# Attention and two gated layers on one core: weights rounded from 8 bytes with fewer VectorE and more ScalarE operations, and a written issue order for the whole program

## The chip, the cores and the metric

The kernel runs on one core of one Trainium2 chip. The metric is the device time of one execution in microseconds, from runs of the whole program. The engines are TensorE (matrix products, PE in the profile), VectorE (DVE), ScalarE (ACT), GpSimd (POOL) and SyncE (SP, which issues most transfers). Each engine executes its own instructions in the order in which they were issued, and engines wait for each other by semaphores.

## The reference

Three stages follow each other. The first is attention with a window of 128 positions and a linear distance bias, for 4 sequences of 576 positions and 8 heads of 64; its result is read as 2304 tokens of width 512. The second is a gated layer of inner width 1536, the third a product of two projections of inner width 1024, a square matrix and an output matrix.

```python
x = attention(q, k, v)                        # 2304 x 512
gate = 1.0 / (1.0 + np.exp(-(x @ w_gate)))
x = gate * (x @ w_val) @ w_out                # inner width 1536
a = x @ w1
b = x @ w2
h = a * b @ w3                                # inner width 1024
return (h @ w_out2).astype(np.float32)
```

The weights arrive as 8-byte floating-point numbers; the kernel takes each apart as two 4-byte words, `low` and `high`, and makes a 4-byte number of them. That is called a rounding below. Every operand of a large product is then split in a high part and a remainder, and each product is three matmuls (high x high, high x remainder, remainder x high).

## The kernel before, in words

The 2304 tokens are five blocks of 2, 4, 4, 4 and 4 tiles of 128. The attention phase runs over 20 steps (5 blocks x 4 pairs of heads) as a pipeline written for TensorE: scores (`stage_s`, L817), then on the other engines mask (L826), bias (L830), maximum (L838, L842), exponentials on ScalarE (L846), sums and reciprocals (L850, L851), normalizing (L856 on GpSimd, L858 on ScalarE); then transposes (`stage_p`, L867) with a copy to SBUF on ScalarE (L106, tile `cp`) and masks on GpSimd (L873, L877); then the product with the values (`stage_pv`, L892). Steps 2 and 3 take their keys and queries from one tile, `boot`, which three transfers fill (L787 to L789). Between the steps TensorE gets pieces of the second stage (`fill`).

The second stage runs over 12 slices of the inner width in groups of two, and for each group over the blocks: the products gate and value (`gv`, L422), a tanh (L437), the gated product on VectorE (L444), its split on ScalarE and GpSimd (L106, L112), then the output product (`dn`, L462) with its addition on VectorE (L470, L472). The third stage first folds `w3` and `w_out2` into one matrix (L383), keeps it in DRAM, and then forms the products by a scheme with seven block products in place of eight (`products`, L533), with operands made by `form_part` and `x_forms`, and the output (`down2`, L663).

Weights are fetched by SyncE (L172, L175) into a ring, rounded by `rounded` (L197 on ScalarE, L199 to L204 on VectorE) and either split into a weight tile (`c`), kept as a form, or stored to DRAM as 4 bytes for later (L217). 76 pieces of 128 x 512 weights are rounded.

Three things set the order. TensorE's order in the attention phase is the program's. The order of the other four engines in the attention phase and shortly after it is written out in the strings of `TURNS`: one letter per instruction, and `line_up` ties each instruction to the one before it in the string. Letters are e for an exponential, n for normalizing, p for the copy of transposes, o for the split of a value product, m, t, x, s for mask, bias, maximum and sum, a and r for the rounding's ScalarE and VectorE instructions, c for the weight's split, g, y and d for tanh and gated product, its split, and the addition; on SyncE k, b, v, w and u for the transfers of keys and queries, `boot`, values, weights, and stores. After the attention phase a scheduler orders every engine by priorities (`high_priority`, `issue_after`).

Of the kernel before, what the change touches and what calls it, by code (L numbers as in the profile page):

```python
# [27 lines left out]
F64_LEAST = 0x38000000  # L28
F64_MOST = 0x47EFFE00
# [9 lines left out]
        "hhmtxmtxsxsrmrtrxsxsrmtrxsxsrmmtsosrxtrxrmsosrtmsxsxtrxrsxrsomrtosxsxmtrxrsxsrrmsstoxmxtgxxrssrm"  # L39
        "sstmxtxorssrmsstmxoxtrxrsmsxotmxsrsxrtrxrxsrsrromstmxrsgddxdtrxrsxrdsrmrtsmsxortrxrgsrsrsmsodddt"  # L40
        "mxtxrdrxrsxrsmotsmsxtxrxrrxsrsrmormgsdddstdrxrxtrxrmrxrsrsrtosxgsmddtsxdssmstoxmxtxxsmsdtomxsxst"
        "ssxxmotxgsdxmdtsdsdsxxsosgdddoorrdrdddgrdrrrrgdrdrrrddgdddd"
    ),
    mybir.EngineType.Activation: (
        "khThhThhaeeeeennepepeaeneehnpepeeeeocnnnnppoeeeepeeeeapnnonneeeepeopeeenngnneepeeceeeneopnnancpe"
        "eeeeeeeopnnnnpeeeeepeeennnnyopaeeeepoceeenneagneeneeepeoeepcnnannyepeeeeneeoenpgnnecepeepeeeenon"
        "nnapeoeeepyeeeenannngpeeeeeoeeenpnnanyeeeppeeoeegneneeenneppeeeeonnnnpeeeeoeepnneegnenepeeypneen"
        "oeeeyeeenngenpeoeepnnnppyooagcaccycgccygy"
    ),
    mybir.EngineType.Pool: (  # L50
        "hhhihhhhhhhhhhhhhThiTnnzzzznnzzhTnzznTnnTzzzczznzznznnTTnzznzTnnzzncnnznzzczzTnnnnzzTzznznnnTzyz"
        "zznncznnnzTzncnnzzznzynnnzzzznnzncnzTzzznzynnnznzTTzTnznnznynznnzzzzznnnnznznzzznnznnyzznznnznzy"
        "znznzzzzycccyccycy"
    ),
    mybir.EngineType.SP: (
        "kkkkkbwbbkvwkvvvkkkwkkvkvkwkkvkwkvvkkkwwvkvkkwkkvkkvuwvkkkuwkkkvuukvkvvvkvwwwwww"
# [26 lines left out]
def attn_moe_kernel(  # L83
# [106 lines left out]
    def rounded(t, key):  # L190
# [89 lines left out]
    def form_part(i, c, x):  # L280
# [3 lines left out]
        def split(at, src):  # L284
            hi, lo = w[:, at : at + 2, 0], w[:, at : at + 2, 1]
            act_copy(hi, src)
            pool_lo(lo, src, hi)
# [845 lines left out]
```

## Time and profile before

| | before |
|---|---|
| median of 3 runs | 879.13 us (879.13 to 880.4) |
| span of the profiled execution | 878.4 us |
| TensorE busy | 863.3 us, 4448 matmuls |
| VectorE busy | 654.0 us, 1161 instructions |
| ScalarE busy | 349.1 us, 853 instructions |
| GpSimd busy | 300.1 us, 357 instructions |
| TensorE idle in the first 88 us | 10.5 us |

The span runs from the first to the last instruction of one profiled execution; the runs' time is taken around the whole execution, and their median stands 0.7 us above it. A line of an engine's busy time tells how much of the span it worked; which engine set the end is read from what TensorE waited for and from the windows.

### The profile page before, as it was taken

What the parts mean: (1) busy time and instruction counts of PE and PEld (TensorE: products, weight loads), DVE (VectorE), ACT (ScalarE), POOL (GpSimd) and SP (SyncE); (2) the same over time, 40 slices, a digit from 0 to 9 for tenths busy, and PEclk for the clock granted to TensorE, in tenths of its full rate; (3) what the DMA queues carried; (4) which work ended last, traced back from release to release, by engine and by line L of the source; (5) the groups of instructions that cost most, each with busy time, mean ns of one, the idle gap of its engine ahead of it and who ended that gap; (6) DMA issues with size and microseconds to landing.
All of it is one profiled execution on the core that took longest, in us unless ns stands there. A gap on an engine that the chain in (4) does not pass through costs nothing.

```text
span 878.4 us, 12512 instructions
## 1 busy us (share of the span) xinstructions
PE 863.3 (98%) x4448; PEld 713.4 (81%) x4448; DVE 654.0 (74%) x1161; ACT 349.1 (40%) x853; POOL 300.1 (34%) x357
## 2 busy tenths in 40 slices
PE   6999999999999999999999999999999999999998
PEld 4677777788888888888888788888888888888887
DVE  6999996699988986993999955873558877643445
ACT  6998776433223223322322333432433334222110
POOL 4877555544135123313311211122555431111120
PEclk8999999999999999999999999999999999999999
DMA  5545540423722430530355421158325355654322
GB/s 186 174 160 179 179 154 16 144 95 115 244 74 83 151 127 24 170 132 1 105 191 168 159 85 54 67 180 318 137 84 180 109 216 216 217 179 155 134 82 97
DMA packets 40767, 121.67 MB, mean 139 GB/s; under 512 B 4480, under 2 KB 6784, under 8 KB 38656
## 3 DMA queue, kind: packets, MB, share of 16 engines
q1 hardware_dynamic: 39264, 105.92, 35.7%
q10 hardware_dynamic: 1440, 14.94, 4.0%
q8 instruction: 35, 0.57, 0.3%
q14 instruction: 28, 0.23, 0.1%
HBM read 88.34 MB, written 32.51 MB: 138 GB/s over the span
## 4 chain that ended last, share of the span: by engine, by line
PE 86%; DVE 6%; DMA 3%; issue 1%; ACT 1%; POOL 1%; SPq 0%; ACTq 0%; DVEq 0%
PE gv L422 28%; PE dn L462 15%; PE o L663 11%; PE pb L533 10%; PE pd L533 5%; PE w3o L383 5%; PE pv L892 3%; PE s L817 3%; PE lone L632 3%; PE pc L533 2%; PE pt L867 2%; DMA boot<-in_q_dram 1%; DVE acc L472 1%; DMA aw_('ahead', 15, 0)_4822<-in_w_dram 1%; DMA _('ahead', 'w3', 4)_5168<-in_w_dram 1%
## 5 line engine op out<-in xcount | busy, mean ns | idle before, releaser
L422 PE MATMUL gv<-xth,wsl 128*128 128x512 f32 (+1 forms) x960 | 279.6, 370 | 1.5 <-DVE g L444 1.5
L422 PEld LDWEIGHTS gv<-xth,wsl 128*128 128x128 f32 x960 | 174.6, 188 | 35.6 <-DVE g L444 2.1
L422 PE MATMUL gv<-xtl,wsl 128*128 128x512 f32 (+1 forms) x480 | 176.8, 368 | 0.0
L112 POOL TENSOR_TENSOR gt<-g,gt 128x512 fp32r<-128x512 f32 (+1 forms) x60 | 74.6, 1246 | 246.1 <-ACT gt L106 241.2
L462 PE MATMUL dn<-gt,wsl 128*128 128x512 f32 (+1 forms) x720 | 155.1, 369 | 0.4 <-DVE g L444 0.4
L462 PEld LDWEIGHTS dn<-gt,wsl 128*128 128x128 f32 x720 | 125.8, 189 | 24.3 <-ACT sm L858 0.7
L422 PEld LDWEIGHTS gv<-xtl,wsl 128*128 128x128 f32 x480 | 90.5, 189 | 14.6
L533 PE MATMUL pb<-xf,forms 128*128 128x512 f32 x384 | 97.7, 391 | 0.0
L472 DVE TENSOR_TENSOR acc<-acc,dn 128x512 f32<-128x512 f32 (+1 forms) x120 | 73.5, 625 | 16.7 <-PE dn L462 16.6
L533 PEld LDWEIGHTS pb<-xf,forms 128*128 128x128 f32 x384 | 70.8, 188 | 14.8 <-ACT xa L106 0.5
L106 ACT ACTIVATE gt<-g 128x512 fp32r<-128x512 f32 (+1 forms) x60 | 35.1, 586 | 78.7 <-DVE g L444 78.7
L846 ACT ACTIVATE sm<-sm,mn 128x128 f32<-128x128 f32 x144 | 56.0, 392 | 10.1 <-DVE mn L842 8.5
L673 DVE TENSOR_TENSOR acc<-acc,o 128x512 f32<-128x512 f32 (+1 forms) x54 | 36.5, 678 | 31.3 <-PE o L663 31.2
L444 DVE SCALAR_TENSOR_TENSOR g<-g,gv 128x512 f32<-128x512 f32 (+1 forms) x60 | 37.4, 627 | 29.3 <-PE gv L422 29.0
L533 PE MATMUL pd<-xf,forms 128*128 128x512 f32 x192 | 48.8, 389 | 0.0
L663 PE MATMUL o<-outw,tp 128*128 128x512 f32 x192 | 48.0, 390 | 0.0
L663 PE MATMUL o<-outw,tq 128*128 128x512 f32 (+1 forms) x192 | 47.6, 386 | 0.0
L112 POOL TENSOR_TENSOR tp<-x,tp 128x512 fp32r<-128x512 f32 x15 | 20.5, 1367 | 78.9 <-ACT tp L106 78.8
L437 ACT ACTIVATE g<-gv 128x512 f32<-128x512 f32 (+1 forms) x60 | 32.0, 547 | 32.3 <-PE gv L422 25.6
L383 PE MATMUL w3o<-wo,w3s 128*128 128x512 f32 x192 | 44.0, 389 | 0.0
L663 PEld LDWEIGHTS o<-outw,tp 128*128 128x128 f32 x192 | 36.0, 188 | 8.0 <-DVE tp L109 0.3
L533 PEld LDWEIGHTS pd<-xf,forms 128*128 128x128 f32 x192 | 36.0, 188 | 7.5
(808 smaller groups left out, 1445.7 us busy)
## 6 DMA issues: line engine op xcount, KB each, us to landing
formd<-forms ACTq DMA_DIRECT2D x8, 1792.0 KB, 6.0
outw<-outd SPq DMA_DIRECT2D x16, 512.0 KB, 5.0
forms<-formd SPq DMA_DIRECT2D x8, 1024.0 KB, 5.1
ldk<-in_k_dram SPq DMA_DIRECT2D x16, 320.0 KB, 2.9
ldv<-in_v_dram SPq DMA_DIRECT2D x16, 320.0 KB, 3.7
out_dram<-acc SPq DMA_DIRECT2D x17, 256.0 KB, 2.0
ldq<-in_q_dram SPq DMA_DIRECT2D x16, 256.0 KB, 3.9
outd<-w3o SPq DMA_DIRECT2D x8, 512.0 KB, 2.9
```

The costliest lines, as they stand in the source:

```text
L106: return nc.scalar.activation(dst, src, AF.Copy)
L112: nc.gpsimd.tensor_tensor(dst, src, hi.bitcast(F32), ALU.subtract)
L383: nc.tensor.matmul(acc2, w3s[u][:, wp, i * P : (i + 1) * P], wo2[kk][:, xp], start=(kk == 0 and wp == 0 and xp == 0), stop=(kk == NC2 - 1 ...
L422: nc.tensor.matmul(ps, wsl[i][:, s, wp, kk * P : (kk + 1) * P], xs[blk][xp][:, kk], start=(kk == 0 and wp == 0 and xp == 0), stop=(kk == N ...
L437: nc.scalar.activation(g[i], pss[i, 0], AF.Tanh, scale=0.5)
L444: nc.vector.scalar_tensor_tensor(pr, pr, 1.0, pss[i, 1], ALU.add, ALU.mult)
L462: nc.tensor.matmul(ps, wsl[i][:, 2, wp, m * P : (m + 1) * P], t[:, xp], start=n == 0, stop=n == 3 * len(grp) - 1,)
L472: nc.vector.tensor_tensor(a, a, ps, ALU.add)
L533: nc.tensor.matmul(ps, forms[i][:, a, wp, kk * P : (kk + 1) * P], xf[n, j][:, xp, kk], start=first and kk == 0 and (wp, xp) == PASSES[0], ...
L663: nc.tensor.matmul(ps[:, c], ts2[n, i][blk][:, xp, tt * P : (tt + 1) * P], outw[i][:, wp, c], start=k == 0, stop=k == 3 * len(grp) - 1,)
L673: nc.vector.tensor_tensor(a, a, ps[:, c], ALU.add)
L846: nc.scalar.activation(y, y, AF.Exp, bias=mn[:, j : j + 1], scale=1.0 / up, accum_out=sums[:, j, 0:1])
```

## The change

The rounding is rewritten: the scaling of the high word and the scaling of the low word are each one ScalarE operation, and VectorE clamps, joins the sign and joins the two words. The second temporary gets two buffers (`bufs=2`), the ring of 4-byte weights three instead of four. All instructions after the attention phase get letters too (F, X, P, L, D, f, K, O, A, Z, l and more of the old ones; q, r, R and j belong to the rounding), the strings run to the end of the program, and `line_up` is called there. TensorE's order is the program's all the way. The scheduler's priorities and `issue_after` give way to the letters.

```diff
-F64_LEAST = 0x38000000
-F64_MOST = 0x47EFFE00
+MOST = 0x0FEFFE00
+LOW_SCALE = 7.49 * 2.0**-32
...
     mybir.EngineType.Activation: (
-        "khThhThhaeeeeennepepeaeneehnpepeeeeocnnnnppoeeeepeeeeapnnonneeeepeopeeenngnneepeeceeeneopnnancpe"
+        "kThhhhTeeheeheenneejpapncnapoeeepejeeeennonnppppeeeeeeeneonnoneeeeppeeeennnceneeepegeeeponnjjnnppaee"
+        "eeeeneenconnppeeeeeeeennoynnaeepeeeopeeeanjnngeeneppeeoeneejcnncnjyppaeeeeeeeenonganneepepeoeceeejnn"
...
     mybir.EngineType.SP: (
-        "kkkkkbwbbkvwkvvvkkkwkkvkvkwkkvkwkvvkkkwwvkvkkwkkvkkvuwvkkkuwkkkvuukvkvvvkvwwwwww"
+        "kkbkkkbbwvvkwkkvvwkkkwvkkvkkvkkvwkkvvwkkvwkvkkwkkwukvkwkkkvukvukkuvkvkkvvvwwwwwwwwwwwwwwwuwuwwuuwwuu"
...
         a = (capool or spool).tile([P, DM], U32, name=f"a_{key}", tag="ca", bufs=rings["ca"])
-        s = spool.tile([P, DM], U32, name=f"s_{key}", tag="cs", bufs=1)
-        x, y = a.bitcast(F32), s.bitcast(F32)
+        s = spool.tile([P, DM], U32, name=f"s_{key}", tag="cs", bufs=2)
+        x = a.bitcast(F32)
         with turn("a"):
-            nc.scalar.activation(x, high.bitcast(F32), AF.Abs)
+            nc.scalar.activation(x, high.bitcast(F32), AF.Copy, scale=2.0**-112)
+        with turn("j"):
+            nc.scalar.activation(s, low, AF.Copy, scale=LOW_SCALE)
+        with turn("q"):
+            nc.vector.tensor_scalar(x, x, -bits(MOST), bits(MOST), ALU.max, ALU.min)
         with turn("r"):
-            nc.vector.tensor_scalar(x, x, bits(F64_LEAST), bits(F64_MOST), ALU.max, ALU.min)
-            nc.vector.tensor_scalar(a, a, 0x07FFFFFF, 3, ALU.bitwise_and, ALU.logical_shift_left)
-            nc.vector.scalar_tensor_tensor(a, high, 0xC0000000, a, ALU.bitwise_and, ALU.bitwise_or)
-            nc.vector.tensor_scalar(s, a, 0xFF800000, None, ALU.bitwise_and)
-            nc.vector.scalar_tensor_tensor(y, low, 2.0**-52, y, ALU.mult, ALU.mult)
-            nc.vector.tensor_tensor(x, x, y, ALU.add)
+            nc.vector.scalar_tensor_tensor(s, high, 0x80000000, s, ALU.bitwise_and, ALU.bitwise_or)
+        with turn("R"):
+            nc.vector.scalar_tensor_tensor(a, a, 3, s, ALU.logical_shift_left, ALU.bitwise_or)
...
-    rings.update({"raw": 3, "raw32": 4, "ca": 4})
+    rings.update({"raw": 3, "raw32": 3, "ca": 4})
...
+    ctx.enter_context(tc.manual_schedule(engines={mybir.EngineType.PE}))
     fillers += [layer(groups[0], 4), layer(groups[1], 3), layer(groups[1], 4)]
...
     while queue:
         convert_next()
-    line_up()
...
     for _ in downs:
         pass
+    line_up()
```

## Rows read from the trace of the kernel before

**Rows 1.** The page: busy us (share) and instructions; speed of transfers in 40 slices.
```profile
PE 863.3 (98%) x4448; PEld 713.4 (81%) x4448; DVE 654.0 (74%) x1161; ACT 349.1 (40%) x853; POOL 300.1 (34%) x357
...
GB/s 186 174 160 179 179 154 16 144 95 115 244 74 83 151 127 24 170 132 1 105 191 168 159 85 54 67 180 318 137 84 180 109 216 216 217 179 155 134 82 97
```
**Rows 2.** Windows of 22 us: each engine's busy us (instructions), granted clock, DMA share, GB/s.
```profile
0.00:22.00 22.00, 13.95 (x70) 9.29 (x71) 13.78 (x32) 13.78 (x53) 10.68 (x41) 0.84 0.56 186
22.00:44.00 22.00, 20.53 (x153) 15.02 (x153) 21.27 (x55) 21.39 (x83) 19.43 (x38) 1.00 0.51 175
44.00:66.00 22.00, 21.36 (x155) 15.52 (x155) 21.28 (x52) 21.17 (x81) 17.41 (x31) 1.00 0.45 159
66.00:88.00 22.00, 21.65 (x174) 17.53 (x175) 21.61 (x54) 19.18 (x69) 16.49 (x26) 1.00 0.54 180
```
**Rows 3.** Windows of TensorE alone, in two long stretches.
```profile
150.00:480.00 330.00, 330.00 (x1616) 1.00 0.35 119
506.00:862.00 356.00, 356.00 (x1670) 1.00 0.41 148
```
**Rows 4.** TensorE's waits: total us, times, longest.
```profile
PE s L817 <- DMA boot<-in_q_dram: 3.8, 1, 3.8
...
PE gv L422 <- DVE g L444: 1.5, 1, 1.5
```
**Rows 5.** The chain that ended last: start us, us, what.
```profile
216.15 5.44 PE dn L462 x24
221.59 10.88 PE gv L422 x48
```
**Rows 6.** TensorE's timeline in the attention phase: start us, us, line, tiles, count, idle before.
```profile
11.23 2.08 PE L817 MATMUL s<-boot 64*128 64x256 f32 x8 [3.76 <-DMA boot<-in_q_dram]
...
43.15 1.03 PE L867 MATMUL pt<-ident,sm 128*128 128x128 f32 x8
...
48.26 0.66 PE L867 MATMUL pt<-ident,sm 128*128 128x128 f32 x2
49.17 1.51 PE L867 MATMUL pt<-ident,sm 128*128 128x128 f32 x6 [0.24 <-POOL sm L856]
...
72.81 0.62 PE L462 MATMUL dn<-gt,wsl 128*128 128x256 f32 x3 [0.35 <-DVE g L444]
```
**Rows 7.** VectorE's timeline near 480 us.
```profile
477.74 0.42 DVE L199 TENSOR_SCALAR _('ahead', 'w3', 9)_5234<-_('ahead', 'w3', 9)_5234 128x512 f32<-128x512 f32 x1
...
479.35 0.69 DVE L201 SCALAR_TENSOR_TENSOR _('ahead', 'w3', 9)_5234<-_('ahead', 'w3', 9)_5204,_('ahead', 'w3', 9)_5234 128x512 uint32<-128x512 uint32 x1
...
483.11 1.52 DVE L200 TENSOR_SCALAR a_('w3', 6)_5562<-a_('w3', 6)_5562 128x512 uint32<-128x512 uint32 x1
484.55 0.68 DVE L204 TENSOR_TENSOR _('ahead', 'w3', 9)_5234<-_('ahead', 'w3', 9)_5234,_('ahead', 'w3', 9)_5235 128x512 f32<-128x512 f32 x1
485.15 0.67 DVE L444 SCALAR_TENSOR_TENSOR g<-g,gv 128x512 f32<-128x512 f32 x1
```
**Rows 8.** GpSimd's timeline at the same place.
```profile
482.73 1.61 POOL L112 TENSOR_TENSOR gt<-g,gt 128x512 fp32r<-128x512 f32 x1 [14.78 <-ACT gt L106]
```
**Rows 9.** ScalarE's first weight instruction, and VectorE's first maximum.
```profile
7.56 0.69 DVE L838 TENSOR_REDUCE mn<-sm 128x4 f32<-128x512 f32 x1
...
9.57 0.66 ACT L197 ACTIVATE a_(0, 0)_208<-raw_(0, 0)_129 128x512 f32<-128x512 f32 x1 [4.67 <-DMA raw_(0, 0)_129<-in_w_gate_dram]
10.14 0.39 ACT L846 ACTIVATE sm<-sm,mn 128x128 f32<-128x128 f32 x1
```
**Rows 10.** ScalarE's busy time from its first exponential to 22 us.
```profile
10.14:22.00 11.86, 10.22 (x45) 0.71 0.43 144
```
**Rows 11.** SyncE's timeline: start us, us of the issue, line, tile.
```profile
3.60 0.47 SPq L175 DMA_DIRECT2D raw_(0, 0)_129<-in_w_gate_dram  x1
```
**Rows 12.** The chain that ended last: the last boot transfer.
```profile
4.59 6.40 DMA boot<-in_q_dram
```
**Rows 13.** ScalarE's waits for transfers: total us, times, longest.
```profile
ACT _('ahead', 'w3', 2)_5170 L197 <- DMA _('ahead', 'w3', 2)_5144<-in_w_dram: 7.8, 1, 7.8
```

More of the change, by code (lines that the diff above doesn't have):

```diff
@@ L285, in split @@
             hi, lo = w[:, at : at + 2, 0], w[:, at : at + 2, 1]
-            act_copy(hi, src)
-            pool_lo(lo, src, hi)
+            with turn("F"):
+                act_copy(hi, src)
+                pool_lo(lo, src, hi)
         split(A11 if c == 0 else A21, x)
@@ L308, in keep @@
         r = (i - NF) * P
-        nc.scalar.dma_start(formd[r : r + P, :], forms[i][:, 1:].rearrange("p b h c -> p (b h c)").bitcast(F32))
+        with turn("K"):
+            nc.scalar.dma_start(formd[r : r + P, :], forms[i][:, 1:].rearrange("p b h c -> p (b h c)").bitcast(F32))
     def out_tile(i):
@@ L473, in down1 @@
             if last:
-                act_copy(x2[blk][0][:, m], a)
-                dve_lo(x2[blk][1][:, m], a, x2[blk][0][:, m])
+                with turn("X"):
+                    act_copy(x2[blk][0][:, m], a)
+                    dve_lo(x2[blk][1][:, m], a, x2[blk][0][:, m])
             yield 3 * len(grp) * (cols(blk) / 2.4 + 13.3)
@@ L558, in products @@
         with now():
-            copied = act_copy(x1, b)
+            act_copy(x1, b)
         if n == 0 and i == NF + 1:
-            make_forms(i + 1, copied)
+            make_forms(i + 1)
         while late:
-            with now(), tc.issue_after(copied.ins):
+            with turn("L"):
                 late.pop(0)()
@@ L569, in products @@
         with now():
-            copied = act_copy(x2a, b)
+            act_copy(x2a, b)
         if n == 0:
-            with tc.issue_after((copied if i > NF + 1 else folded[NM - 1]).ins):
-                keep(i)
+            keep(i)
         yield 2
@@ L576, in products @@
         with now():
-            copied = act_copy(x2b, b)
-            added = nc.vector.tensor_tensor(x2b, x2b, d, ALU.add)
+            act_copy(x2b, b)
+            nc.vector.tensor_tensor(x2b, x2b, d, ALU.add)
         while rests:
-            with tc.issue_after(added.ins):
-                rests.pop()()
+            rests.pop()()
         if n == 0 and NF + 1 < i < NF + NM - 1:
-            make_forms(i + 1, copied)
+            make_forms(i + 1)
         yield 0
@@ L592, in products @@
             nc.vector.tensor_tensor(x1, x1, b, ALU.mult)
-            ts[PAIRED[n][0]] = turn(x1, "tp", dve_lo if n and final else pool_lo)
+            ts[PAIRED[n][0]] = turned(x1, "tp", dve_lo if n and final else pool_lo)
         yield 1
@@ L611, in products, with make_forms @@
         yield 1
-    def make_forms(i, after):
-        with tc.issue_after(after.ins):
-            waiting.pop(i)()
+    def make_forms(i):
+        waiting.pop(i)()
         for c in range(2):
@@ L635, in lone @@
                     )
-            with tc.high_priority(offset=SOONER):
+            with turn("l"):
                 if s == 0:
@@ L668, in down2 @@
                     a = acc[blk][:, tt, c]
-                    with tc.high_priority(offset=SOONER):
+                    with turn("D"):
                         if grp[0] == NF:
@@ L675, in down2 @@
                         r0 = (STARTS[blk] + tt) * P
-                        (nc.scalar if c.start else nc.sync).dma_start(out[r0 : r0 + P, c], a)
+                        with turn("Z"):
+                            (nc.scalar if c.start else nc.sync).dma_start(out[r0 : r0 + P, c], a)
                 yield
```

73 lines of the change are left out of this document (47 added, 26 removed).

## Prediction

> **What bounds the kernel now.** I read the busy shares first, then the windows, then what TensorE waited for, then the places themselves. TensorE is busy 863.3 us of a span of 878.4, VectorE 654.0 [rows 1]: 15.1 us of TensorE's span are idle, so nothing that only relieves VectorE can bring more than about that. The windows say where the 15.1 us lie. From 150 to 480 us and from 506 to 862 us TensorE has no idle time [rows 3]. In the first 88 us the four windows leave it 8.05, 1.47, 0.64 and 0.35 us [rows 2], 10.5 in sum; one wait of 1.5 us lies near 485 us [rows 4]; the last 3 us are the tail (the last matmul, its addition, the last store), which the change leaves alone.
>
> A busy TensorE is not always at its pace, since the ends of matmuls are modelled; the pace is seen where a block repeats: 48 matmuls of 512 columns in 10.88 us [rows 5], 226.7 ns each. All the later blocks keep it. In the attention phase they do not: a block of eight transposes takes 1.03 us at 43.15, and from 48.26 to the end of its second row at 50.68 us where two of the eight ran ahead [rows 6], 1.3 us more. There are six such places between 20 us and the last of them at 72.81 us [rows 6]. Counted from start to start against an undisturbed block of the same kind they cost 0.9, 1.5, 1.0, 1.3, 0.8 and 0.6 us, 6.1 us in sum, of which only a part shows as idle.
>
> So what can be won lies in three places: the boot transfer at the start (3.8 us of waiting [rows 4]), these six stalls, and the one wait at 485 us. In the stretch of the stalls VectorE is busy 21.27, 21.28 and 21.61 us of 22 and ScalarE 21.39, 21.17 and 19.18 [rows 2]: both are nearly full, and the change moves work from one to the other.
>
> **The change, part by part.**
>
> *The rounding.* An undisturbed VectorE instruction of the forms at L199, L200 and L202 takes 0.42 us, one of L201, L203 and L204 0.69 us [rows 7]: six of them 3.33 us. The new three are one of the first kind (the clamp, same form as L199) and two with two inputs (same form as L201): 0.42 + 0.69 + 0.69 = 1.80 us. Each rounding gives VectorE back 1.53 us. Seven of the 76 roundings lie in the first 88 us: 7 x 1.53 = 10.7 us there. The other 69 give back 106 us, in stretches where TensorE is not idle at all [rows 3]: that is worth nothing unless it removes the wait at 485 us.
>
> *The added ScalarE instruction.* The conversion of the low word has no row of its own (whole-number input and output). The nearest row is the one beside it, which reads every second word of the same source: 0.66 us [rows 9]; queued behind another, an instruction starts some 0.1 us before the end of the one before, 0.57 us net. I take 0.57 to 0.68 us. Whether converting the type costs more no row shows; that it costs less is excluded by the same 512 elements per partition. Off the start it is hidden: 69 x 0.66 = 46 us, of ScalarE's time after 88 us that is mostly idle. At the start it is not. By the order strings the changed kernel has, when the 88th of the 144 exponentials has been issued, 9 first instructions (a), 9 of the new ones (j) and 6 copies of rounded weights (c) behind it, 24 in all, where the kernel before has 8 and 6. Ten more are 5.7 to 6.8 us on an engine that has 0.61 + 0.83 + 2.82 = 4.3 us free from 22 to 88 us [rows 2].
>
> *ScalarE's head start.* Before, the first thing behind the set-up on ScalarE is the rounding's first instruction; it waits 4.67 us for its weights and the exponentials stand behind it until 10.14 us, though the maximum that the first of them needs is ready at 8.25 us [rows 9]. In the new string four exponentials stand ahead of any weight: 1.9 us gained. Between 10.14 and 22 us ScalarE is busy 10.22 of 11.86 us [rows 10], 1.6 us free. Free in all: 4.3 + 1.9 + 1.6 = 7.8 us; taken: 5.7 to 6.8 us. The attention chain can come forward by 1.0 to 2.1 us where ScalarE is the limit, by more where VectorE was.
>
> *SyncE's order.* The first weight slice (512 KB) was issued at 3.60 us [rows 11], ahead of the last two boot transfers, the last at 4.59 us and landing 6.40 us later [rows 12]. Now all three boot transfers stand ahead of it, one of them between the loads of the first two steps. The last one is issued one slot (0.5 us) earlier with 512 KB less ahead of it. If transfers land in order, that is worth up to 1.6 us more at 318 GB/s, the fastest of the page's slices [rows 1]; if they share the engines, nothing. I take 1.2 us for both (bounds 0 and 2.1). The loads of the second step come one slot (0.5 us) later; VectorE is still at the first step then, which hides it. The weights land no earlier than before, and VectorE needs them later.
>
> *The stalls.* VectorE has 10.7 us more, SyncE brings the boot step 1.2 us sooner, ScalarE allows 1.0 to 2.1 us. Ends: nothing (ScalarE eats it) and 6.1 + 2.1 = 8.2 us (all six stalls and the boot). I take 2.5 us, near ScalarE's end, as it is the engine whose load grows.
>
> *The wait at 485 us.* TensorE waits 1.54 us for the gated product (L444) at 485.15 us. It stands in VectorE's queue behind L200, 1.52 us long where others take 0.42, and L204, 0.68 us [rows 7]. Both instructions are gone in the changed kernel. 2.2 us ahead of it against a wait of 1.5: I take the whole 1.5 us. Ends: 0 and 1.54.
>
> The long L200 started at 483.11 us, while a GpSimd subtraction ran from 482.73 for 1.61 us [rows 8]; it ended 0.3 us after that one, as if it had stood still. The Trainium skill (SBUF — State Buffer, section "Who interferes with whom") says that VectorE's two-port forms, and its instructions with two SBUF inputs, share a port pair with GpSimd, and that the loser blocks for the whole of the other's instruction; the row agrees (1.10 us lost). By that rule the three new instructions can all still be blocked, and the wait at 485 us would keep up to 1.1 us.
>
> *The order of everything else.* TensorE's own order is the program's in both: before, 24 dn and 48 gv follow each other as the loops are written [rows 5]. For the other engines the order after the attention phase was the scheduler's and is now a string. The buffers for 4-byte weights go from four to three, so the second load of a pair waits one form longer; the second temporary of the rounding lets two roundings overlap. With no idle time on TensorE from 506 to 862 us there is nothing to win there, only to lose: bounds 0 and the loss of the third rival. I take 0.
>
> *Sum.* 878.4 - 2.5 - 1.5 = 874.4 us of span. The median of the runs, 879.13, stands 0.7 us above the profiled span; with it 875.1 us.
>
> **The rivals.**
>
> *VectorE was the limit alone* (0.13). All six stalls and the boot's 2.1 us go, with the wait at 485: 6.1 + 2.1 + 1.5 = 9.7 us, 869.4 us. For it: VectorE's 21.3 to 21.6 of 22 us. Against it: ScalarE is as full.
>
> *Half the wait at 485 stays* (0.09). One of the new instructions is blocked beside GpSimd ahead of L444 as L200 was: 1.1 us come back, 876.2 us.
>
> *ScalarE takes VectorE's place* (0.18). Its ten more instructions use all that is free up to the 88th exponential; stalls move from 20 to 73 us to 65 to 95 us and nothing is won there. Only the wait at 485 goes: 877.6 us. The point from which it decides: an added instruction of over 0.75 us, or exponentials that don't start before 10 us.
>
> *A weight instruction at the head of ScalarE's queue* (0.16, slower). After the attention phase ScalarE's order is now fixed, with two instructions per load (a and j) instead of one that must wait for a transfer. Before, such waits reached 7.8 us [rows 13] and cost nothing, because the tanh that empties a bank had 10.88 us of matmuls ahead of it [rows 5] and the scheduler could place around them. Where the string puts tanh (g) or the gated copies (y) behind a load that lands later than that, TensorE stands still. It decides when wait and queue together pass some 10 us. Four such places at the price of the one in the trace, 1.54 us, are 6.2 us: 878.4 - 2.5 + 6.2 - 1.5 + 0.7 = 881.3 us. For it: the one wait of before is of this kind, at the end of the densest run of weights. Against it: VectorE's queue, which caused that one, gets shorter.
>
> **How the numbers follow.** The forecast 875.1 us gets 0.44 (its own range 872 to 877.3), the rivals 0.13, 0.09, 0.18 and 0.16. About 0.2% (1.8 us) is what a measurement here can tell from no change: faster is below 877.4 us. Faster: 0.44 + 0.13 + 0.09 = 0.66; same: 0.18; slower: 0.16. The range reaches from the large gain to the slower case, 869.5 to 881.0 us; outside are about half of each, 0.07 and 0.09.
>
> **What would show it.** Right: VectorE's busy time near 654 - 76 x 1.53 = 538 us or a little below, ScalarE's near 349 + 76 x 0.66 = 399; the boot step's matmuls near 10.0 us (11.23 before [rows 6]); the first exponential near 8.3 us; the transposes' blocks of 48 us at 1.0 us each; no wait for L444 near 480 us; TensorE still without idle time from 150 to 860 us. Wrong: an added ScalarE instruction above 0.75 us; ScalarE at 22 of 22 us from 44 to 88 us with TensorE waiting for it; any new wait of TensorE after 150 us; a boot step that starts at 11 us again.

## The result, and the profile after

The change made the kernel slower: 886.31 us (885.88 to 888.29, 4 runs) against 879.76 us (879.13 to 880.44), a ratio of 1.0076 with a 95% interval of 1.0062 to 1.0091. Forecast were 875.1 us and a range up to 881.0 us.

The page of the changed kernel, busy time and instructions of each engine, to be read beside [rows 1]:

```profile
span 886.6 us, 12284 instructions
...
PE 869.8 (98%) x4448; PEld 715.4 (81%) x4448; DVE 538.4 (61%) x933; ACT 387.5 (44%) x929; POOL 299.1 (34%) x357
```

VectorE lost 115.6 us of work, as forecast (538 us busy), and the span grew by 8.2 us. The profiled execution is the slowest of the four of the changed kernel; between the medians the loss is 6.6 us. Less work and more time can both be true only if VectorE's work was not what TensorE waited for. What TensorE did wait for (total, times, longest), to be read beside [rows 4]:

```profile
PE pt L891 <- POOL sm L880: 6.7, 8, 1.3
PE s L841 <- DMA ldk<-in_k_dram: 3.8, 1, 3.8
PE pb L559 <- ACT xa L119: 1.0, 2, 0.7
```

The wait for the boot transfer (3.8 us) and the one for the gated product near 485 us (1.5 us) are both gone. In their place stand eight waits of TensorE's transposes for the normalized exponentials (`sm`, L880), 6.7 us, all in the attention phase. The windows, to be read beside [rows 2] and [rows 3] (columns as there):

```profile
0.00:22.00 22.00, 15.95 (x60) 9.67 (x62) 12.03 (x25) 13.56 (x48) 11.62 (x42) 1.00 0.64 206
22.00:44.00 22.00, 19.83 (x146) 13.48 (x142) 17.45 (x45) 20.02 (x83) 15.62 (x35) 1.00 0.47 153
44.00:66.00 22.00, 18.98 (x148) 13.62 (x147) 19.00 (x43) 20.11 (x72) 14.36 (x28) 0.92 0.51 172
66.00:88.00 22.00, 22.00 (x170) 18.04 (x172) 20.21 (x48) 21.10 (x73) 17.25 (x30) 1.00 0.44 149
480.00:506.00 26.00, 26.00 (x139) 22.55 (x138) 10.12 (x16) 6.60 (x12) 5.15 (x4) 1.00 0.00 1
506.00:862.00 356.00, 354.81 (x1662) 296.81 (x1661) 205.63 (x316) 120.23 (x219) 98.00 (x76) 1.00 0.46 164
```

From 22 to 66 us VectorE is idle for 4.6 and 3.0 us of each window where it was idle for 0.7 before, ScalarE for 2.0 and 1.9 where it was idle for 0.6 and 0.8: no engine is full, and TensorE still idles more. From 480 to 506 us it is never idle. From 506 to 862 us, where it had no idle time, 1.2 us appear.

One landmark serves for all kernels below: a block of 16 score matmuls near the end of the attention phase. It starts at 121.02 us in the kernel before and at 128.35 us in the changed one:

```profile
121.02 2.00 PE L817 MATMUL s<-ldk,ldq 64*128 64x256 f32 x16
```
```profile
128.35 2.00 PE L841 MATMUL s<-ldk,ldq 64*128 64x256 f32 x16
```

So 7.3 us are lost by then. The wait near 485 us gives back 1.9 us (measured below). The last matmuls stand 7.7 us later than before (882.17 against 874.48 us), so 2.3 us are lost again in between. The rest of the 8.2 us, 0.5 us, lies behind the last matmul.

**Where the first loss begins.** VectorE's timeline of the changed kernel (start, us, line, tiles, and the idle time before with what ended it):

```profile
13.14 0.16 DVE L874 TENSOR_REDUCE su<-summed 128x4 f32<-128x8 f32 x1 [2.22 <-ACT sm L870]
13.22 0.69 DVE L850 COPY_PREDICATED s<-mask,s 128x512 f32<-128x512 int32 x1
...
22.10 0.70 DVE L850 COPY_PREDICATED s<-mask,s 128x512 f32<-128x512 int32 x1 [1.17 <-PE s L841]
...
23.32 0.68 DVE L850 COPY_PREDICATED s<-mask,s 128x512 f32<-128x512 int32 x1
23.91 0.15 DVE L874 TENSOR_REDUCE su<-summed 128x4 f32<-128x8 f32 x1
```

The boot step's scores begin at 8.29 us, but their mask stands behind the sum of step 1, which waits 2.22 us for ScalarE; the mask runs at 13.22 us, where it ran before (13.35). Later the sum of step 2 stands behind the masks of step 4, and these wait for TensorE's scores. ScalarE at the same time:

```profile
16.34 0.63 ACT L119 ACTIVATE wsl<-a_(0, 0)_208 128x512 fp32r<-128x512 f32 x1 [1.29 <-DVE a_(0, 0)_208 L218]
...
17.17 0.65 ACT L210 ACTIVATE a_(0, 1)_316<-raw_(0, 1)_131 128x512 f32<-128x512 f32 x1
18.82 0.38 ACT L119 ACTIVATE cp<-pt 128x256 f32<-128x256 f32 x1 [1.00 <-PE pt L891]
...
19.36 0.40 ACT L870 ACTIVATE sm<-sm,mn 128x128 f32<-128x128 f32 x1
```

The split of the rounded weight waits 1.29 us for VectorE, a copy waits 1.00 us for TensorE, and the exponentials of step 2 behind both start at 19.36 us (16.41 before). TensorE's transposes of that step start at 25.27 us (22.73 before):

```profile
19.99 2.93 PE L841 MATMUL s<-ldk,ldq 64*128 64x256 f32 x16
...
25.27 0.90 PE L891 MATMUL pt<-ident,sm 128*128 128x128 f32 x4 [1.24 <-POOL sm L880]
...
51.07 0.33 PE L891 MATMUL pt<-ident,sm 128*128 128x128 f32 x1 [0.70 <-POOL sm L880]
52.72 2.02 PE L891 MATMUL pt<-ident,sm 128*128 128x128 f32 x7 [1.32 <-POOL sm L880]
```

The last two rows are step 7's. An engine that executes its queue in order stands still for an instruction that nobody needs yet, while one that TensorE needs is ready behind it. That is the theory. The Trainium skill (PSUM — Partial Sum Buffer, section "Engine vs sequencer instructions") says that the queues of ScalarE, VectorE and GpSimd are strictly first in, first out; the 2.22 us agree with it.

The first row shows a rival for a part of this first loss, TensorE's own pace: step 4's sixteen score matmuls take 2.93 us, 2.00 us in the kernel before (at 18.91 us) and 2.00 us for the next sixteen (at 27.55 us). So up to 0.9 us of the delay of VectorE's masks is TensorE's pace and not a queue, though the clock column reads 1.00 for the first 22 us. No run separates the two.

### The profile page after: what moved, and what is told of

Its sections match the earlier page's. It is cut to its first block, busy times and chain, and to the rows that moved or that the text cites. A ratio compares the mean times of both kernels' runs of the same rounds, so it can differ in the third digit from the quotient of the medians.

```text
span 886.6 us, 12284 instructions
## 1 busy us (share of the span) xinstructions
PE 869.8 (98%) x4448; PEld 715.4 (81%) x4448; DVE 538.4 (61%) x933; ACT 387.5 (44%) x929; POOL 299.1 (34%) x357
## 5 line engine op out<-in xcount | busy, mean ns | idle before, releaser
L445 PE MATMUL gv<-xth,wsl 128*128 128x512 f32 (+1 forms) x960 | 279.4, 370 | 0.0
L445 PEld LDWEIGHTS gv<-xth,wsl 128*128 128x128 f32 x960 | 174.8, 189 | 33.4 <-issue 2.0
L445 PE MATMUL gv<-xtl,wsl 128*128 128x512 f32 (+1 forms) x480 | 176.9, 369 | 0.0
L445 PEld LDWEIGHTS gv<-xtl,wsl 128*128 128x128 f32 x480 | 90.6, 189 | 14.7
L559 PE MATMUL pb<-xf,forms 128*128 128x512 f32 x384 | 98.2, 391 | 1.0 <-ACT xa L119 1.0
L559 PEld LDWEIGHTS pb<-xf,forms 128*128 128x128 f32 x384 | 71.1, 188 | 15.5 <-ACT xa L119 1.6
L559 PE MATMUL pd<-xf,forms 128*128 128x512 f32 x192 | 48.7, 389 | 0.0
L559 PEld LDWEIGHTS pd<-xf,forms 128*128 128x128 f32 x192 | 36.1, 188 | 7.5
L404 PEld LDWEIGHTS w3o<-wo,w3s 128*128 128x128 f32 x192 | 36.1, 188 | 7.5
```

Source lines behind the costliest of these rows:

```text
L404: nc.tensor.matmul(acc2, w3s[u][:, wp, i * P : (i + 1) * P], wo2[kk][:, xp], start=(kk == 0 and wp == 0 and xp == 0), stop=(kk == NC2 - 1 ...
L445: nc.tensor.matmul(ps, wsl[i][:, s, wp, kk * P : (kk + 1) * P], xs[blk][xp][:, kk], start=(kk == 0 and wp == 0 and xp == 0), stop=(kk == N ...
L559: nc.tensor.matmul(ps, forms[i][:, a, wp, kk * P : (kk + 1) * P], xf[n, j][:, xp, kk], start=first and kk == 0 and (wp, xp) == PASSES[0], ...
```

## The experiments

Two theories. *Load*: the engines' added or removed work (VectorE less, ScalarE more) decides how late a step is. *Order*: the order of the queues decides, and the load only where it stands ahead of something that TensorE waits for. The landmark is that of 121.02 us above. Ratios are to the kernel before in runs on the same chip. The strings in the diffs are shown in pieces.

| kernel | median, us | ratio (95%) | landmark, us |
|---|---|---|---|
| e1_round_only | 882.78 | 1.0036 (1.0023 to 1.0049) | 122.38 |
| e2_new_early | 884.85 | 1.0054 (1.0039 to 1.0069) | 128.04 |
| e3_new_late | 886.61 | 1.0080 (1.0065 to 1.0095) | 123.39 |
| e4_boot_first | 881.18 | 1.0014 (1.0005 to 1.0023) | 122.05 |
| e5_sum_first | 885.00 | 1.0054 (1.0041 to 1.0068) | 126.54 |
| e6_no_low_word | 884.55 | 1.0050 (1.0034 to 1.0065) | 128.60 |
| e7_old_round_new_early | 911.32 | 1.0359 (1.0345 to 1.0373) | 148.95 |
| e8_new_round_after | 877.95 | 0.9976 (0.9967 to 0.9985) | 120.83 |
| e10_repaired_start | 886.99 | 1.0081 (1.0065 to 1.0096) | 131.06 |
| e11_after_early_boot | 882.20 | 1.0029 (1.0017 to 1.0042) | 127.10 |
| e12_two_repairs | 891.24 | 1.0136 (1.0122 to 1.0150) | 134.77 |
| e13_after_tensor_fixed | 884.02 | 1.0051 (1.0038 to 1.0064) | 120.49 |
| e14_tensor_free | 891.80 | 1.0144 (1.0130 to 1.0158) | 126.43 |
| e15_old_order_no_low_word | 877.62 | 0.9975 (0.9966 to 0.9984) | 120.00 |
| e16_j_late | 887.26 | 1.0091 (1.0077 to 1.0104) | 129.77 |

A landmark comes from one execution. Kernels that have the same attention phase show how well it repeats: 121.02, 120.83 and 120.49 us (before, e8, e13), 122.38 and 123.39 us (e1, e3), 128.35, 128.04 and 126.43 us (the changed kernel, e2, e14). So a difference of 2 us or less between two landmarks is not told apart.

Of the expectations below, nine kernels fell outside the ranges of both theories: e1, e4, e7, e10, e11, e12, e13, e14 and e16. The theory of the order says afterwards where the time went; how much a change of order costs it did not foretell.

### One part alone: e1, e2, e3, e4

e1 is the kernel before with the new rounding and the smaller ring: in its strings each group of six r becomes q, r and R at the places of the first, third and sixth, and j stands behind each a. After the attention phase the scheduler orders, as before.

```diff
-        "hhmtxmtxsxsrmrtrxsxsrmtrxsxsrmmtsosrxtrxrm
+        "hhmtxmtxsxsqmtrxsxsmtxsxsRmmtsosqxtxrm
...
-        "khThhThhaeeeeennepepeaeneehn
+        "khThhThhajeeeeennepepeajeneehn
```


> The new rounding (two ScalarE, three VectorE operations, the second temporary with two buffers, the ring of 4-byte weights with three) in the old issue order: in the strings each new instruction stands where one of the old rounding stood, the added ScalarE instruction right behind the first; one ScalarE rounding instruction at the very end of the strings is moved behind two weight copies, which the smaller ring needs; the scheduler orders the rest as before. Theory 'order' (the loss lies in the new order of the attention phase): 877.5 to 880.5 us, the wait at 485 us gone or kept. Rival 'ScalarE' (the added ScalarE instruction costs it, whatever the order): 883 to 887 us, with TensorE waiting in the attention phase as in the changed kernel.

e2 is e1 with the new strings for the attention phase. e3 has the attention order of e1 and the new strings and TensorE's program order afterwards.

```diff
-        "hhmtxmtxsxsqmtrxsxsmtxsxsRmmtsosqxtxrm
+        "hhmtxmtxsxssmsrqtRmxtxxoxmqmststsxsxorRm
```


> The new rounding and the new strings cut at the point where the old ones ended (the attention phase and the first two groups' rest); from there on the scheduler orders as before. Theory 'order of the attention phase': 884.5 to 887 us, with the same waits of TensorE for GpSimd's normalizing before 120 us as the changed kernel. Rival 'late order' (the written order after the attention phase costs the time): 878 to 881 us.

> The changed kernel with the old order of the attention phase (as in the first kernel of this call) and the new strings for all that follows. Theory 'order of the attention phase': 877.5 to 881 us. Rival 'late order': 883 to 887 us. Rival 'ScalarE': 883 to 887 us too, but then the first kernel of this call is as slow.

e4 is the kernel before, with the boot transfers ahead of the first weight slice on SyncE.

```diff
-        "kkkkkbwbbkvwkvvv
+        "kkbkkkbbwkvwkvvv
```


> The kernel before with one thing changed: SyncE issues the three boot transfers ahead of the first weight slice, as the new string does (the first nine letters of SyncE's string). If the boot transfer was what the start waited for: 877 to 878.5 us, and the first matmul of the boot step at 8.5 to 9.5 us in place of 11.23. If the start is bound by VectorE and ScalarE behind it, or by the exponentials behind the first weight slice: 879 to 880.5 us with the boot step early and nothing won.

At the landmark the new rounding in the old order (e1) is 1.4 us behind the kernel before; the new order with the same rounding (e2) is 7.0 us behind. So 5.7 us come with the order of the attention phase; the 1.4 us of the rounding in the old order are within what the landmark repeats by. The order is here that of four engines, SyncE's transfers among them. In the traces of e2 and of the changed kernel TensorE waits for a transfer, behind its first load, only 1.0 and 0.5 us, but no run keeps SyncE's old order beside the other new strings, so its share is open. In medians the later strings cost 3.8 us on top of e1 (e3, which came out where its rival had it) and 1.5 us on top of e2 (the changed kernel).

e1 loses 3.3 us more at one place, which the changed kernel does not have; e3 has it too, with a wait of 3.8 us for the same addition where e1 waits 1.94 us, so a part of e3's 3.8 us lies here and not in the later strings. TensorE's waits there, and SyncE's timeline ahead of it:

```profile
171.91 0.97 PE L463 MATMUL dn<-gt,wsl 128*128 128x512 f32 x3 [1.94 <-DVE acc L471]
177.24 2.60 PE L463 MATMUL dn<-gt,wsl 128*128 128x512 f32 x10 [0.70 <-POOL gt L112]
```
```profile
155.55 0.43 SPq L172 DMA_DIRECT2D raw_(2, 1)_2133<-early  x1
164.87 0.32 SPq L172 DMA_DIRECT2D raw_(3, 1)_2138<-early  x1
```

The fourth load of 4-byte weights is issued 9.3 us after the third, where the kernel before issued it 0.5 us after. That fits the ring of three, and e8, e15 and e16 with a ring of four have no such wait. But the changed kernel, also with three, issues its fourth load 6.3 us after the third (168.01 and 161.69 us), and TensorE does not wait there. The ring alone does not make the wait, and the kernel before with a ring of three alone was not tried: this is argued and not shown.

In e4 the boot step's scores start at 10.42 us, but the first weight now lands later, and its instruction stands ahead of the exponentials on ScalarE:

```profile
11.50 0.66 ACT L197 ACTIVATE a_(0, 0)_208<-raw_(0, 0)_129 128x512 f32<-128x512 f32 x1 [6.60 <-DMA raw_(0, 0)_129<-in_w_gate_dram]
12.06 0.38 ACT L846 ACTIVATE sm<-sm,mn 128x128 f32<-128x128 f32 x1
```

The first exponential comes at 12.06 us against 10.14 [rows 9]: a transfer 0.8 us sooner for TensorE made ScalarE 1.9 us late.

### Load or order: e6, e7, e15, e16

e6 takes ScalarE's added instruction out of the attention strings of e2.

```diff
-        with turn("j"):
+        if marked is None:
             nc.scalar.activation(s, low, AF.Copy, scale=LOW_SCALE)
...
-            nc.vector.scalar_tensor_tensor(s, high, 0x80000000, s, ALU.bitwise_and, ALU.bitwise_or)
+            if marked is None:
+                nc.vector.scalar_tensor_tensor(s, high, 0x80000000, s, ALU.bitwise_and, ALU.bitwise_or)
+            else:
+                nc.vector.scalar_tensor_tensor(s, high, 0x80000000, high, ALU.bitwise_and, ALU.bitwise_and)
```


> As e2_new_early, but the twelve roundings inside the attention strings leave out the added ScalarE instruction (the low word is not computed, the VectorE instruction with the sign reads the high word twice), so ScalarE has about 12 x 0.66 us less in its queue and VectorE the same. Theory 'the added ScalarE instructions fill ScalarE': most of what e2 lost against e1 and before comes back, 880.5 to 882.5 us. Theory 'order of the strings': the stalls are made by instructions that wait for another engine at the head of a queue, and 884 to 885 us stay.

It gains nothing (884.55 against 884.85 us): ScalarE's added work in the new order is not the cause.

e15 takes VectorE's load away and leaves the order: the strings and the ring of the kernel before, three VectorE and one ScalarE operations in the attention phase, the full new rounding afterwards.

```diff
-        "hhmtxmtxsxsrmrtrxsxsrmtrxsxsrmmtsosrxtrxrm
+        "hhmtxmtxsxsqmtrxsxsmtxsxsRmmtsosqxtxrm
```


> The order and the four buffers of the kernel before, everything after the attention phase as in e8_new_round_after (877.95 us); the twelve roundings of the attention strings are done by three VectorE instructions and the one ScalarE instruction of before (the low word is not computed, the VectorE instruction with the sign reads the high word twice). VectorE has 10 us less in the first 88 us and nobody has more. Theory 'VectorE's load makes the stalls of the attention phase' (the prediction's term A, and its rival that VectorE is the limit alone): 872 to 876 us. Theory 'the stalls are chains from engine to engine, not load': 877.3 to 878.5 us.

It is the decisive run. Its windows, columns as in [rows 2]:

```profile
22.00:44.00 22.00, 20.62 (x159) 15.33 (x159) 19.27 (x47) 21.18 (x82) 18.53 (x37) 1.00 0.53 189
44.00:66.00 22.00, 21.24 (x159) 15.54 (x157) 19.56 (x49) 21.44 (x85) 16.41 (x31) 1.00 0.45 157
66.00:88.00 22.00, 21.94 (x168) 17.27 (x165) 19.92 (x44) 18.42 (x65) 17.02 (x28) 1.00 0.55 178
```

VectorE has 2.0, 1.7 and 1.7 us less in the three windows than in [rows 2], ScalarE the same within 0.8, and TensorE's busy time is 20.62, 21.24 and 21.94 us against 20.53, 21.36 and 21.65. The median, 877.62 us, is that of e8 (877.95), which has the old rounding in the attention phase. VectorE's 21.3 of 22 us were no limit: relieving it is worth at most the 0.8 us at the landmark, and nothing that the times can tell.

e7 is the other way round: the old six operations in the new attention order, in two lumps of three.

```diff
-        "hhmtxmtxsxssmsrqtRmxtxxoxmqm
+        "hhmtxmtxsxssmsrrrtrrrmxtxxoxmrrrm
```


> The six VectorE and one ScalarE operations of the kernel before in the rounding, everywhere, but the attention phase in the order of the new strings (the two halves of the six operations put where the new string has the first and the last of the three; the added ScalarE instruction has no place); the order after the attention phase is the scheduler's and the buffers are those of before. Theory 'order': the new order alone makes the loss, 884 to 888 us (VectorE has more in it than in e2). Theory 'the new rounding makes the loss': 879 to 881 us, as the order then costs nothing.

In the new order the old rounding costs 26.5 us more than the new (911.32 against 884.85 us), far outside both expectations. So load is not free in every order; that it counts where it stands ahead of what TensorE waits for is argued, since e7 changes the load and what stands ahead at once. A part is not VectorE's: TensorE stands still for 6.1 us ahead of its scores at 102.34 us. Between a load of keys at 82.41 us and a weight load at 98.18 us SyncE issues nothing, and the load of queries stands behind the weight load, at 98.57 us. The profile does not name what ended TensorE's wait; that it was these queries is argued.

e16 adds the low word to e15, with j as late in ScalarE's string as the third VectorE instruction allows, and that one (r) directly ahead of R.

```diff
-        "hhmtxmtxsxsqmtrxsxsmtxsxsRmm
+        "hhmtxmtxsxsqmtxsxsmtxsxsrRmm
```


> The new rounding everywhere, low word included, in the order and with the four buffers of the kernel before; in the attention strings the added ScalarE instruction stands as late as the third VectorE instruction allows, and not beside the first ScalarE instruction as in e1_round_only (882.78 us). Theory 'a rounding instruction costs only what it holds up behind it': as e15_old_order_no_low_word, or up to 1 us more. Theory 'ScalarE's load': 878.5 to 880 us, since ScalarE has 0.66 us more for each rounding.

Both expectations missed: 887.26 us. VectorE's timeline shows why:

```profile
70.87 0.69 DVE L203 SCALAR_TENSOR_TENSOR s_(1, 1)_767<-raw_(1, 1)_336,s_(1, 1)_767 128x512 uint32<-128x512 uint32 x1 [1.07 <-ACT s_(1, 1)_767 L199]
```
```profile
76.97 0.63 PE L463 MATMUL dn<-gt,wsl 128*128 128x256 f32 x3 [1.48 <-DVE g L445]
```

VectorE stands at r for 1.07 us until ScalarE has done j; the gated product (L445) comes later by that and by the rounding behind it, and TensorE waits 1.48 us. e16 is 9.6 us behind e15, which lacks the added instruction. The fairer comparison is e1, which has the same rounding with j early: at the landmark e16 is 7.4 us behind it (129.77 against 122.38 us), with the same work in another order. e1 also has two buffers for the second temporary where e16 has one; in the rows above j itself waits for no buffer, it stands behind exponentials.

### The places in the new order: e5, e10, e12, e11

e5 is e2 with the sum of step 2 ahead of the masks of step 4.

```diff
-        "hhmtxmtxsxssmsrqtRmxtxxoxmqmststsxsxorRm
+        "hhmtxmtxsxssmsrqtRmxtxxoxssmqmttsxsxorRm
```


> As e2_new_early (884.85 us), but in VectorE's string of the attention phase the sum and the reciprocal of step 2 stand ahead of the masks of step 4, as in the kernel before, instead of behind them. Theory 'sum behind mask' (VectorE's queue waits for TensorE's scores of step 4 while a finished step 2 waits for its sum): the second half's transposes of step 2 come about 1.4 us earlier than in e2 (24.9 us there) and the median falls to 883.4 to 884.0 us. Theory 'ScalarE is the limit' (the eight-byte instructions stand ahead of step 2's exponentials): the exponentials of step 2 are late anyway, the transposes move by under 0.4 us and the median stays at 884.5 to 885.2 us.

The transposes move from 24.89 to 24.01 us, more than the second theory allowed and less than the first; the median does not move. The profiled execution's landmark is 1.5 us earlier than e2's, but it was also the fastest of its runs (883.49; the others 884.86 to 885.22), so this is not counted; most of it is a stretch at half clock, from 52.3 to 55.7 us, which e2's execution has and this one has not (last section).

e10 repairs the whole start of e2: the boot step's mask ahead of the sum of step 1, and the exponentials of steps 2 and 3 ahead of the split of the weight.

```diff
-        "hhmtxmtxsxssmsrqtRmxtxxoxmqmststsxsxorRm
+        "hhmtxmtxsxsmtxsxsrmtxqsxsRomqmttsxsxorRm
...
-        "kThhhhTeeheeheenneejpapncnapoeeepejeeee
+        "kThhhhTeeheeheenneejpnnpeeeeapeeeepnnocaj
```


> As e2_new_early, but the start of the strings is repaired: VectorE does the boot step's mask, scores and maximum (step 2) ahead of the sum of step 1, those of step 3 ahead of the second and third rounding instruction, and the sum of step 2 ahead of the masks of step 4; ScalarE does the exponentials of steps 2 and 3 ahead of the copy of the rounded weight; GpSimd's subtraction of that weight stands behind the normalizing of step 2. Theory 'the start's order': in e2 the transposes of step 2 begin at 24.9 us against 22.7 in before, here at 21.5 to 23.0, and of the 4.2 us by which e2 is behind before after 100 us some 2 to 3 go: 881.8 to 883.2 us. Theory 'the stalls at 48 us and later eat it': whatever is gained at 25 us is lost by 60 us and 884.5 to 885 us stay.

The transposes of step 2 came at 23.18 us, near what the first theory expected (24.89 in e2), and the median rose to 886.99 us, which neither theory had. The next step took the stall; GpSimd's timeline, VectorE's and TensorE's:

```profile
27.28 0.72 POOL L857 TENSOR_SCALAR sm<-sm,su 128x128 f32<-128x128 f32 x2 [2.44 <-DVE su L852]
```
```profile
22.35 0.69 DVE L827 COPY_PREDICATED s<-mask,s 128x512 f32<-128x512 int32 x1
23.10 1.47 DVE L201 TENSOR_SCALAR a_(0, 1)_316<-a_(0, 1)_316 128x512 f32<-128x512 f32 x1
24.50 0.68 DVE L827 COPY_PREDICATED s<-mask,s 128x512 f32<-128x512 int32 x1
...
26.29 0.14 DVE L851 TENSOR_REDUCE su<-summed 128x4 f32<-128x8 f32 x1
```
```profile
27.71 1.25 PE L868 MATMUL pt<-ident,sm 128*128 128x128 f32 x4 [3.40 <-POOL sm L857]
```

The sum of step 3 (26.29) stands behind two masks and a rounding instruction of step 4's time; TensorE waits 3.40 us. e12 repairs step 7 as well: ScalarE's three weight instructions and VectorE's third rounding go behind that step's exponentials and sums.

```diff
-        "onnjjnnppaeeeeeeneenconnppeeee
+        "onnnnppeeeeeeneenonnjjappeeeec
```


> As e10_repaired_start, with the second place repaired too: ScalarE's three weight instructions ahead of the exponentials of step 7 stand behind them, VectorE's third rounding stands behind the sums of step 7. Theory 'each place costs what stands ahead of the step that TensorE waits for': the transposes of step 7 begin 1 to 2 us earlier against e10, no stretch at half clock follows at 53 us, and the median is 1 to 2.5 us below e10's. Theory 'a common limit further on': the same median as e10 within 0.6 us.

Step 7's first transpose comes sooner, as expected (51.87 us, 53.40 in e10), and the median is 4.3 us worse: step 8's start at 63.87 us, where e10 had 62.30. The granted clock has a part in it: it is 0.51 from 60.0 to 70.5 us, in e10 only from 56.8 to 60.3 us. In both kernels the repair of one step moved the stall to the next. That the order of the attention strings costs the time is shown by e1 and e2; which places in it do is not, since putting right the places named above brought nothing back.

e11 brings the early boot to e8, with the boot step's mask at once behind step 1's first work.

```diff
-        "hhmtxmtxsxsrmrtrxsxsrmtrxsxsrmm
+        "hhmtxmtxsxsmtxxrrrssrmtrxsxsrmm
...
-        "khThhThhaeeeeennepepeaeneehn
+        "khThhThheeeeennepepeaaeneehn
...
-        "kkkkkbwbbkvwkvvvkkkwkkvkvkw
+        "kkbkkkbbwvvkwkkvvwkkkwvkkvk
```


> As e8_new_round_after (877.95 us), with the early boot of the new strings: SyncE's new order, the first exponentials ahead of the first weight instruction on ScalarE, and on VectorE the boot step's mask, scores and maximum ahead of the first rounding and of the sum of step 1. Theory 'the early boot is worth its 2 us as soon as no instruction of another step stands ahead of it': the transposes of step 2 begin 1 to 2 us earlier than in before (22.7 us) and the median is 876 to 877 us. Theory 'VectorE and ScalarE are full from 22 to 88 us': the lead is gone by 60 us and 877.7 to 878.3 us stay.

Timeline of TensorE in e11, then in e8:

```profile
9.89 2.08 PE L839 MATMUL s<-boot 64*128 64x256 f32 x8 [1.01 <-DVE s L848]
...
18.80 1.57 PE L839 MATMUL s<-ldk,ldq 64*128 64x256 f32 x12
...
105.34 3.39 PE L839 MATMUL s<-ldk,ldq 64*128 64x256 f32 x16 [2.87 <-DMA ldq<-in_q_dram]
```
```profile
11.20 2.08 PE L839 MATMUL s<-boot 64*128 64x256 f32 x8 [3.57 <-DMA boot<-in_q_dram]
...
18.73 1.57 PE L839 MATMUL s<-ldk,ldq 64*128 64x256 f32 x12
```

A lead of 1.3 us is gone by the scores of step 4: in between, at 17.33 us, TensorE waits 1.44 us for GpSimd's normalizing, where e8 does not wait. So these 1.3 us of the boot wait of 3.8 us [rows 4] were not on the path that sets the end: beside it other engines' work went on that the next steps need. e11's loss comes later, in waits of 0.58 and 0.72 us for ScalarE's normalizing near 67 us and in the one of 2.87 us for a transfer at 105 us. That SyncE's new order beside the old strings makes the last one is argued.

### TensorE's order: e13, e14

e13 is e8 with TensorE's matmuls in the program's order after the attention phase; e14 is the changed kernel without that line.

```diff
     line_up()
+    ctx.enter_context(tc.manual_schedule(engines={mybir.EngineType.PE}))
```


> As e8_new_round_after (877.95 us), but TensorE's matmuls after the attention phase stand in the program's order, as in the changed kernel, instead of the scheduler's; the other engines keep the scheduler's order. Theory 'fixed order of TensorE': the matmuls pb stand in two groups behind each other near 603 and 769 us with nothing between to cover the copy of their operand, TensorE waits 0.2 to 0.75 us at three to five places (as the changed kernel does at 635, 679 and 775 us), 878.6 to 879.6 us. Theory 'the other engines' strings make those waits': 877.7 to 878.3 us.

```diff
-    ctx.enter_context(tc.manual_schedule(engines={mybir.EngineType.PE}))
     fillers += [layer(groups[0], 4), layer(groups[1], 3), layer(groups[1], 4)]
```


> The changed kernel (886.31 us) with its strings for the other engines, but TensorE's order after the attention phase is the scheduler's again. Theory 'TensorE's program order makes the later losses' (e13_after_tensor_fixed lost 6 us by it alone): the waits for xa at 635, 679 and 775 us go, 884.3 to 885.3 us. Theory 'the strings of the other engines make them': 886 to 886.7 us.

e13 lost 6.1 us against e8, all of it after 600 us (at the landmark the two are 0.3 us apart). TensorE in e13:

```profile
600.73 1.52 PE L555 MATMUL pb<-xf,forms 128*128 128x512 f32 x6
...
606.82 1.90 PE L555 MATMUL pb<-xf,forms 128*128 128x512 f32 x6 [3.14 <-ACT xa L108]
```

and in e8 at the same place:

```profile
602.50 1.55 PE L555 MATMUL pc<-xf,forms 128*128 128x512 f32 x6
...
605.20 1.55 PE L555 MATMUL pb<-xf,forms 128*128 128x512 f32 x6
```

In the scheduler's order pc and more of `lone` stand between two pb, and cover the copy of xa. In the program's they come behind. The changed kernel waits for the same tile (xa, L559, 1.0 us). e14, which frees TensorE beside the strings, has the changed kernel's attention phase and ends 5.5 us behind it, against both expectations: a wait of 2.1 us for xa appears at another place (678.72 us). That the strings are fitted to TensorE's program order would explain it. Of the late loss it is shown that TensorE's fixed order alone costs 6.1 us under the scheduler, that with the later strings 1.5 us (against e2) to 3.8 us (against e1) are left, and that freeing TensorE alone does not bring it back. How it divides among the strings stays open.

### A version that beats both: e8

e8 keeps order and ring of the kernel before, and the old rounding in the attention strings; behind them it uses the new one.

```diff
     def rounded(t, key):
+        if marked is not None:
+            return rounded_old(t, key)
```


> The kernel before with its order and its buffers; the twelve roundings of the attention strings stay the old ones, all the later ones are the new three VectorE and two ScalarE operations. Term B of the prediction alone: the wait of 1.5 us for the gated product near 485 us goes and nothing else moves: 877.9 to 878.6 us. Rival: the third buffer of four and the second ScalarE instruction cost nothing, but another wait takes the place of the one that goes (as the wait near 170 us in e1_round_only): 879.5 to 881 us.

877.95 us, a ratio of 0.9976 (0.9967 to 0.9985). VectorE's gated products near 485 us now wait for TensorE and not the other way:

```profile
483.86 0.69 DVE L466 SCALAR_TENSOR_TENSOR g<-g,gv 128x512 f32<-128x512 f32 x1 [7.54 <-PE gv L444]
```

## Why the prediction was wrong, point by point

*Costs of the instructions: right.* VectorE 538.4 us (538 forecast), ScalarE 387.5 us (399 forecast, so 0.51 us net for each added instruction and not 0.66). Two sums are off without deciding anything. Up to the 88th exponential the strings have 20 weight instructions against 13, seven more and not ten; the counts in the prediction hold at the 92nd. And the runs' time stands 1.7 us above the span of the same execution (888.29 and 886.6 us), not 0.7; with that the forecast would have been 876.1 us. The conversion of the low word takes what its neighbour takes:

```profile
44.31 0.68 ACT L212 ACTIVATE s_(0, 2)_328<-raw_(0, 2)_218 128x512 uint32<-128x512 uint32 x1
```

*The wait at 485 us: right.* The term of 1.5 us came: e8 has it alone, 1.9 us in the profiled span and 2.3 us in the median. The rival that half of it stays did not.

*Boot and head start: right as facts, worthless as gains.* The boot step's scores start at 8.29 us (10.0 forecast) and the first exponential at 8.24 us (8.3 forecast). What failed is "I take 1.2 us for both" and "1.9 us gained": a wait in the profile was priced as time on the path to the end. e11 shows a lead of 1.3 us vanish by 18.8 us, and in the changed kernel VectorE's queue spent it at 13.14 us.

*The stalls: wrong in sign, and the step that failed.* "VectorE has 10.7 us more ... I take 2.5 us": the gain was reckoned by adding up free time on engines. Measured is a loss of 7.3 us at the landmark. e15 shows that 5.4 us less VectorE work in these windows bring nothing, e6 that ScalarE's added work is not what costs either, e2 against e1 that the order costs 5.7 us. The order of the attention strings had changed throughout, and the working counted what stood in the strings but not what stood behind what.

*"I take 0" for the order of everything else: wrong, 2.3 us in the profiled execution, 1.5 us between the medians of e2 and the changed kernel.* The sentence that TensorE's order is the program's in both kernels is false behind the attention phase: there the scheduler had moved pc between the pb. A block that repeats the loops [rows 5] does not show that all blocks do; the `manual_schedule` line in the diff said so.

*The rivals.* That a queue's head would wait for something late, with TensorE behind it, was the slower rival's mechanism and is what happened. It was put on ScalarE alone, after the attention phase, and for weights that land late; it happened on VectorE, ScalarE and GpSimd in the attention phase, for results of each other. VectorE as the limit alone is refuted by e15, ScalarE's added work in its place by e6.

## What to carry to other kernels

An engine that is busy for 97% of a stretch need not limit it: take its work away in an otherwise unchanged order before counting on the gain. When an in-order issue string is replaced, compare for each engine what stands ahead of the instruction that the next engine waits for, and count the waits there; sums of busy time said nothing of it here. Repairs of single places in a hand-made order gained nothing here (e5, e10, e12), so an improvement that needs no new order (here the new rounding behind the attention phase, 0.24%) is the one to take first.

## What the runs showed of the hardware

Of TensorE's clock: in the changed kernel the granted clock falls to half, 1.2 GHz, from 52.6 to 56.0 us, at the end of two waits of 0.70 and 1.32 us for step 7; from 44 to 52.6 us and from 56 to 66 us it is full. In e13 it falls from 608.1 to 611.4 us, right behind the wait of 3.14 us. Windows of the changed kernel, then of e13 (the column ahead of the DMA share is the clock):

```profile
52.60:56.00 3.40, 3.28 (x15) 2.26 (x17) 2.61 (x5) 2.50 (x8) 2.16 (x5) 0.50 0.68 245
```
```profile
608.10:611.40 3.30, 3.30 (x10) 2.65 (x9) 0.77 (x2) 0.60 (x1) 0.00 (x0) 0.50 1.08 446
```

In such a stretch TensorE counts as busy, and no row lists the loss as a wait. What it costs the pair of the changed kernel and e14 shows, which have the same attention phase and the same two waits. In e14 the clock stays full (1.00 from 44 to 66 us). From the end of the second wait (52.72 and 52.00 us) to the next score block TensorE needs 4.92 us in the changed kernel and 3.71 us in e14:

```profile
57.64 2.00 PE L841 MATMUL s<-ldk,ldq 64*128 64x256 f32 x16
```
```profile
52.00 1.47 PE L891 MATMUL pt<-ident,sm 128*128 128x128 f32 x7 [1.33 <-POOL sm L880]
...
55.71 2.00 PE L841 MATMUL s<-ldk,ldq 64*128 64x256 f32 x16
```

So a stall can cost more than its own length, here 1.2 us more, and the same stall in another execution cost only itself.

A small VectorE instruction can be long: beside a GpSimd subtraction from 19.64 us for 1.27 us, one of 4 elements per partition took 1.09 us where most others of it take 0.17, and ended 0.03 us after it.

```profile
19.85 1.09 DVE L866 TENSOR_SCALAR mn<-mn 128x4 f32<-128x4 f32 x1
```

The Trainium skill (SBUF — State Buffer, section "Who interferes with whom") has VectorE's two-port forms and GpSimd lock each other out of a shared port pair for a whole instruction; this row agrees. The new rounding is no less exposed to it (up to 1.78 us for L216 where 0.69 is undisturbed), and yet TensorE did not wait near 485 us.
